# DeltaNet then Fourier mixing: odd heads' operands moved to the other half of the partitions, and the first merge done by halves

## The chip, the cores and the metric

The kernel runs on one core of a Trainium2 chip. The metric is device time in microseconds (us) of one execution; lower is better. Each comparison is between executions on the same chip. An execution more than 1.5 % above the fastest of its kernel counts as slow and is left out of the ratios. The kernel before has medians from 784 to 790 us in the different series, so kernels of different series are compared by their ratios, not by their times.

## The reference, cut to what matters

```python
# deltanet: batch 4, heads 8, positions 768, head dim 48
k_n = k / (np.linalg.norm(k, axis=-1, keepdims=True) + 1e-06)
for t in range(S):
    y[:, :, t] = np.einsum('bhd,bhde->bhe', q[:, :, t], state)
    v_old = np.einsum('bhde,bhd->bhe', state, kt)
    state = state + bt[..., None] * np.einsum('bhd,bhe->bhde', kt, vt - v_old)
# then, with x = y as (4, 768, 384):
mixed = np.real(np.fft.fft(np.fft.fft(x, axis=1), axis=2))
u = x + mixed
un = (u - mu) / np.sqrt(var + 1e-06)
out = u + np.maximum(un @ w_ch1, 0.0) @ w_ch2      # w_ch1 384 x 1536
```

The recurrence is computed in chunks of 64 positions, 48 chunks in all (12 per batch element). Within a chunk, R is the keys times the state, U = T B (V - R) with a triangular inverse T, S is the keys times U, and the state grows by S. T comes from inverting 32x32 blocks on VectorE and *merging* pairs of blocks to 64x64 with two small products.

## The kernel before, in the parts that matter

Four chunks form a quad, and two quads (eight chunks) are inverted together and are called a group here; a *load* is one quad's half of the merge. V is transferred for a whole chunk and four heads at once, so head u of a half of the heads always lies in the same 64 partitions:

```python
def fetch(Q, engs, dst, src):
    for c in range(QT):
        for hh in range(2):
            ...
            engs[hh].dma_start(out=dst[64 * hh:64 * hh + CH, c, :, 0:D],
                               in_=src[b, 4 * hh:4 * hh + 4, t0:t0 + CH, :].rearrange("h p d -> p h d"))
```

The second product of U and the merge therefore use only the diagonal tiles (rows and columns of the same half), two of the four 64x64 tiles of TensorE:

```python
for u in range(4):                       # U <- T B (V - R)
    for hh in range(2):
        pr = slice(64 * hh, 64 * hh + 64)
        mm(pu[pr, u], wt[pr, c, u], U[pr, u], True)
act.activation(U, pu, ACT.Copy)

class Merge:
    ...
    def taken(self, step):               # evacuates pj: four ACTIVATEs of 32x256
        for hh in range(2):
            for v in range(2):
                ...
                act.activation(dst, src, ACT.Copy, scale=-1.0 if step == 0 else 1.0)
    def diagonal(self, half):            # two copies of 32x512
        for hh in range(2):
            r = slice(64 * hh + W * half, 64 * hh + W * half + W)
            act.activation(self.wt[r, :, :, W * half:W * half + W], self.Z[r, self.ns], ACT.Copy)
```

After the inversion the first load is merged whole, before chunk 0 begins:

```python
M = Merge(0, 0)
for step in range(2):
    M.products(step, 0); M.products(step, 1); M.taken(step); M.diagonal(step)
scaled(0); run(masks(0)); scaled(1); run(masks(1))
...
for m in range(NCH): ... chain(m) ...
```

## Time and profile before

| | before |
|---|---|
| time, median of 3 (later of 4) | 788.09 us (788.83 us) |
| profiled span, mean granted clock | 784.7 us, 0.970 |
| PE busy | 699.9 us |
| ACT busy | 260.0 us |
| V transfers | 96 of 48 KB |

These are lines of the page of the kernel before: busy time by engine, the chain that ended last, two groups (busy us, mean ns, then idle time of the engine before them and what ended it), and V's transfers.

```profile
PE 699.9 (89%) x7640; PEld 513.0 (65%) x7640; DVE 379.4 (48%) x952; ACT 260.0 (33%) x634; POOL 58.7 (7%) x83
...
PE 48%; DVE 10%; ACT 5%; issue 3%; DMA 0%; SPq 0%; POOL 0%; POOLq 0%; DVEq 0%; ACTq 0%
...
L131 PEld LDWEIGHTS pc<-U,wt 64*64 64x64 f32 x768 | 34.0, 163 | 19.7 <-issue 10.3
...
V<-in_v_dram SPq DMA_DIRECT2D x96, 48.0 KB, 2.4
```

In all such lines ph and po are the MLP's two products (the last line of the reference) and unT and hT their inputs, evacuated by ACT; pj is the merge's product and wt its result, T B; pt, KQT and pg prepare later chunks.

PE is busy 89 %. pc<-U,wt is U's second product, which the change speeds up. Transfers (DMA, SPq) have no share of the chain; but its shares add up to only 66 %, as it could be followed back no further than 254 us, so it says nothing of the time before.

### The profile page before, as it was taken

Reading aid. Unit: us, or ns where it says so; the run is one execution under the profiler, and the core shown is the slowest. Engines: PE = TensorE matmul, PEld = TensorE weight load, DVE = VectorE, ACT = ScalarE, POOL = GpSimd, SP = SyncE. Lnnn points to the kernel's source line nnn. Section 1 sums busy time; section 2 is a strip of 40 time slices with the busy share of each in tenths; the row PEclk is TensorE's granted clock in tenths of the full one; section 3 lists DMA queues with packets and bytes.
Section 4 is the critical chain, followed back from the end, with each engine's and each line's share of the span. In section 5 each row is a group of like instructions: output and inputs, shape, how many; then the busy total and the mean of one; then the engine's idle time right before and its main releaser. Section 6 shows DMA issues by size and latency. Waiting matters only on the chain.

```text
span 784.7 us, 17842 instructions
## 1 busy us (share of the span) xinstructions
PE 699.9 (89%) x7640; PEld 513.0 (65%) x7640; DVE 379.4 (48%) x952; ACT 260.0 (33%) x634; POOL 58.7 (7%) x83
## 2 busy tenths in 40 slices
PE   5852799989988997999989998999999989999997
PEld 4531687867656765786666775776767666677684
DVE  2699766575992598245961119783111146100000
ACT  3741354227436404532152540315312121021120
POOL 8020000010000001010100001010000010100000
PEclk9999999989998999699999999899999999999999
DMA  8651033225320212001202101001000000000000
GB/s 189 163 113 31 7 85 57 46 74 123 87 69 9 38 32 43 16 10 25 50 6 42 32 2 42 1 1 32 12 12 11 12 11 1 20 1 20 11 11 20
DMA packets 82447, 30.75 MB, mean 39 GB/s; under 512 B 77392, under 2 KB 78928, under 8 KB 82368
## 3 DMA queue, kind: packets, MB, share of 16 engines
q1 hardware_dynamic: 78224, 22.31, 13.8%
q0 software_dynamic: 1968, 6.91, 2.7%
q8 instruction: 60, 0.98, 0.5%
q10 hardware_dynamic: 2176, 0.39, 0.3%
q14 instruction: 19, 0.16, 0.1%
HBM read 24.87 MB, written 4.72 MB: 38 GB/s over the span
## 4 chain that ended last, share of the span: by engine, by line
PE 48%; DVE 10%; ACT 5%; issue 3%; DMA 0%; SPq 0%; POOL 0%; POOLq 0%; DVEq 0%; ACTq 0%
PE ph L131 20%; PE po L131 15%; DVE X L131 3%; PE pc L131 3%; DVE A L131 2%; PE pf L131 2%; PE pj L131 2%; ACT A L131 2%; PE pb L131 2%; ACT wt L131 1%; PE pg L131 1%; PE py L131 1%; DVE sm L131 1%; DVE x L131 1%; PE pt L131 1%
## 5 line engine op out<-in xcount | busy, mean ns | idle before, releaser
L131 PE MATMUL ph<-unT,w 128*128 128x256 f32 x864 | 213.8, 395 | 4.5 <-ACT unT L131 2.0
L131 PE MATMUL po<-w,hT 128*128 128x384 f32 x576 | 202.2, 498 | 1.7 <-ACT KQT L131 0.7
L131 PEld LDWEIGHTS ph<-unT,w 128*128 128x128 f32 x864 | 160.3, 193 | 33.7 <-ACT hT L131 3.7
L131 PEld LDWEIGHTS po<-w,hT 128*128 128x128 f32 x576 | 105.7, 191 | 68.2 <-issue 1.5
L131 ACT ACTIVATE hT<-ph 128x256 f32<-128x256 f32 x144 | 54.9, 383 | 179.6 <-PE ph L131 179.3
L131 DVE TENSOR_TENSOR x<-x,po 128x384 f32<-128x384 f32 x24 | 13.2, 552 | 112.5 <-PE po L131 112.4
L131 ACT ACTIVATE U<-pc 128x192 f32<-128x192 f32 x48 | 15.9, 331 | 110.0 <-PE pc L131 98.4
L131 ACT ACTIVATE KQT<-pt 128x256 f32<-128x256 f32 (+1 forms) x82 | 32.0, 419 | 44.9 <-PE pt L131 44.3
L131 PEld LDWEIGHTS pc<-U,wt 64*64 64x64 f32 x768 | 34.0, 163 | 19.7 <-issue 10.3
L131 PE MATMUL pg<-KQT 48*64 48x64 f32 (+1 forms) x1024 | 41.7, 309 | 5.5 <-ACT KQT L131 4.4
L131 PEld LDWEIGHTS pg<-KQT 48*64 48x64 f32 x1024 | 32.1, 178 | 20.4 <-ACT KQT L131 11.2
L131 PE MATMUL pc<-U,wt 64*64 64x48 f32 x768 | 41.2, 253 | 4.7 <-DVE U L131 2.1
L131 DVE TENSOR_TENSOR st<-st,pc 128x192 f32<-128x192 f32 x44 | 15.3, 347 | 61.0 <-PE pc L131 56.8
L131 DVE TENSOR_TENSOR U<-V,pc 128x192 f32<-128x192 f32 x48 | 16.8, 350 | 53.1 <-PE pc L131 52.9
L131 DVE TENSOR_TENSOR A<-X 128x30 f32<-128x30 f32 (+14 forms) x120 | 41.0, 342 | 2.9
L131 DVE TENSOR_TENSOR X<-X,A 128x30 f32<-128x30 f32 (+14 forms) x120 | 39.5, 329 | 2.9
L131 DVE TENSOR_TENSOR x<-x,pb 128x193 f32<-128x193 f32 (+1 forms) x96 | 26.4, 346 | 23.1 <-PE pb L131 23.1
L716 POOL DMA_INDIRECT out_dram<-x,rows_hi x12 | 12.3, 1024 | 335.9 <-DVE x L131 179.9
L131 PE MATMUL pt<-pack,kp 128*128 128x128 f32 x96 | 24.4, 349 | 10.3 <-DMA pack<-k_pack 4.8
L131 PE MATMUL pt<-pack,qp 128*128 128x128 f32 x96 | 23.4, 341 | 11.0 <-DMA qp<-in_q_dram 11.0
L131 PE MATMUL pj<-Z,A 32*64 32x64 f32 x320 | 15.0, 257 | 19.9 <-DVE Z L131 19.6
L131 ACT ACTIVATE A<-pg 128x256 f32<-128x256 f32 (+1 forms) x72 | 25.4, 378 | 21.7 <-PE pg L131 16.6
(125 smaller groups left out, 840.2 us busy)
## 6 DMA issues: line engine op xcount, KB each, us to landing
qp<-in_q_dram SPq DMA_DIRECT2D x96, 48.0 KB, 2.4
V<-in_v_dram SPq DMA_DIRECT2D x96, 48.0 KB, 2.4
kp<-in_k_dram SPq DMA_DIRECT2D x80, 48.0 KB, 2.5
w<-in_moe_w_ch_dram SPq DMA_DIRECT2D x8, 384.0 KB, 3.2
w<-in_moe_w_ch_dram POOLq DMA_DIRECT2D x6, 384.0 KB, 6.4
x<-in_moe_w_ch_dram SPq DMA_DIRECT2D x6, 384.0 KB, 3.7
x<-in_moe_w_ch_dram POOLq DMA_DIRECT2D x4, 384.0 KB, 9.2
out_dram<-x SPq DMA_DIRECT2D x8, 192.0 KB, 2.0
```

The costliest lines, as they stand in the source:

```text
L131: ins = getattr(self.engine, name)(*args, **kwargs)
L716: nc.gpsimd.indirect_dma_start(out=out.rearrange("b s m -> (b s) m"), out_offset=bass.IndirectOffsetOnAxis(ap=rows_hi[:, i:i + 1], axis=0) ...
```

## The change

Its intent: keep the odd heads' V, R and T B in the other half of the partitions. Then an even and an odd head use different tiles, so U's second product and the merges can go round four tiles in place of two. Besides, the first load is merged by halves, with R of chunk 0 issued between, so that the chain starts earlier. The core of the diff:

```diff
-    def fetch(Q, engs, dst, src):
+    def fetch(Q, engs, dst, src, crossed=False):
...
+                if crossed:
+                    for e in range(2):
+                        h0 = 4 * (hh ^ e)
+                        engs[hh].dma_start(out=dst[64 * hh:64 * hh + CH, c, e::2, 0:D],
+                                           in_=src[b, h0 + e:h0 + 4:2, t0:t0 + CH, :].rearrange("h p d -> p h d"))
+                    continue
...
+            if i == 0:                               # in invert(): lengths of odd heads change sides
+                ...
+                dve.tensor_copy(odd, lns.rearrange("p g n -> p (g n)")[:, 1::2])
+                for hh in range(2):
+                    dve.tensor_copy(lns.rearrange("p g n -> p (g n)")[64 * hh:64 * hh + 64, 1::2],
+                                    odd[64 * (1 - hh):64 * (1 - hh) + 64])
...
-                        mm(self.pj[64 * hh:64 * hh + 64, hh, o:o + 64], ...
+                        p = 64 * hh if self.apart else 64 * (hh ^ w)
+                        mm(self.pj[half][p:p + 64, w, 64 * c:64 * c + 64], ...
...
+                    for ws in (slice(0, 2),) if self.apart else (slice(0, 1), slice(1, 2)):
+                        ...
+                        act.activation(dst[:, :, ws], src, ACT.Copy, scale=-1.0 if step == 0 else 1.0)
...
-                act.activation(self.wt[r, :, :, W * half:W * half + W], self.Z[r, self.ns], ACT.Copy)
+            for e in range(2):
+                o = 64 * (hh ^ e) + W * half
+                copy(self.wt[o:o + W, :, e::2, W * half:W * half + W],
+                     self.Z[r, QT * self.lh:QT * self.lh + QT, e::2])
...
-        for u in range(4):
-            for hh in range(2):
-                pr = slice(64 * hh, 64 * hh + 64)
-                mm(pu[pr, u], wt[pr, c, u], U[pr, u], True)
+        for j in range(2):
+            for e in range(2):
+                for hh in range(2):
+                    pr = slice(64 * (hh ^ e), 64 * (hh ^ e) + 64)
+                    mm(pu[64 * hh:64 * hh + 64, e, j], wt[pr, c, 2 * j + e], U[pr, 2 * j + e], True)
...
     first = invert(0, 1)
     advance(first, 4)
+    first_state(0)
...
-    M = Merge(0, 0)
-    for step in range(2): ...
+    M = Merge(0, 0, True)
+    M.products(0, 0); M.products(0, 1); M.taken(0); M.diagonal(0, 0); M.products(1, 0)   # on five lines
+    step = chain(0)
+    advance(step)
...
```

Not shown: the lists that fix what stands in which chunk of the first chain were rewritten too (the masks, for one, stood ahead of chunk 0 and now stand in chunks 1 and 3).

In number: V's transfers double to 192 of half the size, an evacuation has eight ACTIVATEs of 32x128 in place of four of 32x256, the diagonals of a load eight copies of 32x256 in place of four of 32x512, and PE's instructions stay as many.

## The prediction

> **What bounds the kernel now.** I read the page first, then the timeline of the first chain of chunks, then busy time per stage, then the timeline of a late stage. The page says that PE is busy 89% of 784.7 us, and its chain of work that ended last is PE for 48% with ph and po, the channel MLP, in front. That is an average over unlike stages, so I cut the span at the chain's own marks. The windows view (columns: stretch, length, then busy time of PE, PEld, DVE, ACT, POOL with instruction counts, granted clock, DMA share, GB/s):
>
> ```profile
> 80.60:88.30 7.70, 5.39 (x72) 4.30 (x72) 7.02 (x10) 4.66 (x11) 0.00 (x0) 1.00 0.00 0
> 88.30:142.30 54.00, 49.25 (x1077) 42.83 (x1075) 35.44 (x75) 25.07 (x59) 0.00 (x0) 1.00 0.29 60
> ...
> 256.00:330.00 74.00, 66.63 (x1018) 47.96 (x1010) 46.89 (x121) 29.42 (x76) 3.86 (x4) 0.88 0.17 32
> 330.00:633.00 303.00, 294.98 (x3239) 210.20 (x3237) 134.88 (x362) 89.60 (x222) 17.38 (x22) 0.98 0.09 19
> ```
>
> There are four stages that the change touches. Up to 80.6 us: loads and the inversion on DVE. 80.6 to 88.3: the first merge, alone. 88.3 to 142.3: chunks 0 to 11, a chain R -> U -> U's second product -> S -> state, with little to fill it. After that: the chain lies beside the MLP, and from 330 to 633 PE is busy 295 of 303 us. So before 142 us a latency counts, and after 330 us a saving of PE time counts. The timeline of chunk 1 shows the latency (columns: start, duration, engine, operation):
>
> ```profile
> 94.44 0.93 PEld L131 LDWEIGHTS pc<-U,wt 64*64 64x64 f32 x16 [0.64 <-DVE U L131]
> ...
> 95.46 0.93 PEld L131 LDWEIGHTS pj<-A 32*64 32x64 f32 x16
> ...
> 95.58 0.33 ACT L131 ACTIVATE U<-pc 128x192 f32<-128x192 f32 x1 [0.64 <-PE pc L131]
> 96.50 0.52 PEld L131 LDWEIGHTS pc<-U,kp 64*64 64x64 f32 x16
> ...
> 97.11 0.93 PEld L131 LDWEIGHTS pj<-A 32*64 32x64 f32 x16
> ```
>
> The two products that use two tiles (pc<-U,wt and pj) need 0.93 us for 16 weight loads, 58 ns each; S, which goes round four tiles, needs 0.52 us, 33 ns. In a late stage, by the same view:
>
> ```profile
> 540.67 0.32 PEld L131 LDWEIGHTS pc<-U,kp 64*64 64x64 f32 x16
> ...
> 542.54 1.01 PEld L131 LDWEIGHTS pj<-A 32*64 32x64 f32 x32 [0.55 <-ACT A L131]
> ...
> 543.73 1.53 ACT L131 ACTIVATE wt<-pj 32x256 f32<-32x256 f32 x4 [1.41 <-PE pj L131]
> ```
>
> There it is 0.32 us for 16 in four tiles, and 31.5 ns against 20 ns each. So the same change is worth 0.41 us per 16 early and about 0.2 us late.
>
> **What the Trainium skill says.** "TensorEngine Tiling (Array Packing)", section Tiling Modes: with 64x64 there are four tiles, and different tiles can run LdWeights and Matmul in parallel. The trace agrees: 33 ns against 58 ns. The same page, Performance Considerations: tiling speeds up TensorE but not PSUM evacuation, which may become the bottleneck. The trace is made for that: after 1.01 us of pj, ACT takes 1.53 us. "TensorE: Matmul & The Clock Gate", Part 1: the clock is halved while PE has been little used and full after sustained use. The page's clock row does not show it before 157 us, but durations do: the same 16 loads in 0.52 us at 96 us and 0.32 at 540. So I take early durations for the first chain. "DMA: Bandwidth & Descriptors", Rules for kernel authors: splitting a transfer over partition halves brings nothing, since all go through the same DMA engines; issue time is what counts. Here SyncE spends some 0.6 us on each 48 KB issue.
>
> **The change, part by part.**
>
> *U in four tiles.* One instruction group per chunk, 48 in all: 0.93 -> 0.52 us cold. A plain early chunk is now 3.92 us (chunk 2: R at 98.16 to R at 102.08); U's step and ACT's start follow it directly, so it could be 3.5.
>
> *Merging in four tiles, except the first load.* Each load has four groups of 16. In chunk 1, pj delays S by 0.55 us (0.93 against the 0.38 that S otherwise needs after ACT's start) and the next R by 0.40: chunk 1 lasts 4.88. With 0.52 each both delays vanish behind ACT and DVE. But the evacuation gets finer: eight ACTIVATEs of 32x128 instead of four of 32x256, and eight diagonal copies of 32x256 instead of four of 32x512. ACT's 32x256 takes 0.374 us and 32x512 0.628, so I estimate 0.12 us + 1 ns per element, 0.25 for 32x128. One taken(): 1.53 -> 2.0; the diagonals of a load: 2.54 -> 3.0. Per load +1.4 us of ACT, +15 us in all over eleven loads.
>
> *The first load by halves.* Now:
>
> ```profile
> 80.71 1.81 PEld L131 LDWEIGHTS pj<-Z,A 32*64 32x64 f32 x32 [17.11 <-issue]
> ...
> 82.75 1.53 ACT L131 ACTIVATE A<-pj 32x256 f32<-32x256 f32 x4 [18.30 <-PE pj L131]
> ...
> 87.89 1.28 ACT L131 ACTIVATE wt<-Z 32x512 f32<-32x512 f32 x2
> ...
> 89.54 0.96 PEld L131 LDWEIGHTS pc<-U,wt 64*64 64x64 f32 x16 [0.70 <-issue]
> ```
>
> After: pj half 80.7 to 81.65, ACT from 81.85: taken 1.05 and one diagonal pair 0.75, to 83.65; second pj half-step 82.95 to 83.9; R 83.9 to 84.4; U at 84.65; ACT taken 84.1 to 85.15, second diagonal 85.9 (the others on DVE by 86.0). The second product starts at about 86.0 instead of 89.54: 3.5 us. The rest of the merge (taken of the second half about 1.05 us after U, then 0.93 of pj) holds R of chunk 1 to about 89.2, against 93.28: 4.1 us.
>
> *Chunks 1 to 11.* Work that stood ahead of the chain is now inside it, and the whole of DVE's and ACT's order is fixed. I walked each chunk with the early durations:
> - chunk 1: DVE has masks (1.34) and a 2.0 us transpose between U and state, 1.35 more than the chain needs: 4.9 (was 4.87);
> - chunk 2: a whole load's merge, three output parts and a wait for taken(): 5.0 (was 3.92);
> - chunk 3: ACT has U 0.33, diagonals 3.0, split 1.0: about 3.9 (was 4.88);
> - chunk 4: 4.4 (was 4.06); odd chunks 5, 7, 9: five join steps of 0.48, an output add 0.55 and U on DVE: 4.4 each (were 5.82, 4.88, 5.82);
> - 6, 8: 3.7 each (were 3.98, 4.06); 10: 4.0 (3.98); 11: 2.5 (2.73).
> Sum: R of chunk 12 comes at 89.2 + 4.9 + 5.0 + 3.9 + 4.4 + 3 x 4.4 + 2 x 3.7 + 4.0 + 2.5 = 134.5, against 142.28. **First chain: -7.8 us.** I take -7.6 because of the loads below.
>
> *U after chunk 11.* 36 groups x 0.21 = 7.6 us of PE. PE idles little from 330 to 633, more from 142 to 330, and the two-tile groups partly interleave with py. I count 80%: **-6 us**.
>
> *Merges after chunk 11, eight loads.* PE saves 4 x 0.2 per load warm, but a step is a circle pj -> ACT -> pj. Late it is now 1.01 + 1.53 + about 0.2 = 2.8 us (pj at 542.54, 545.32, 548.10); after, 0.66 + 0.1 + 2.0 + 0.2 = 3.0. At 239 to 254 and 308 to 325 us ACT works through copies and takens almost without a pause, and gets 2.8 us more per pair of loads, while slow pj groups of 1.79 us become shorter. **+1.5 us**, uncertain by 2.
>
> *Twice as many V loads.* 96 issues become 192. From SyncE's timeline an issue of 256 rows takes 0.60 us and one of 128 rows 0.43 to 0.47, so each pair costs about 0.28 us more than one: 8 x 0.28 = 2.2 us per quad. At the start V takes 14.14 us of SyncE for 16 issues, and 4.5 more delay the query loads; queries are prepared by 64 us now and would be by 68.5, while DVE inverts until 77: hidden. V of quad 2 was issued from 103.2 to 111.8 and used at 117.86, some 3.5 us of slack; 2.2 more and an earlier use by 1.5 eat it. I count 0 to 2 us, 0.2 above.
>
> *Small parts.* The lengths' three extra copies (of 128x32) and the earlier first state are on DVE at a time when they can be slotted in: nothing.
>
> Sum: -7.6 - 6 + 1.5 = -12.1, so 788.1 -> 776.
>
> **The rivals.**
> 1. *ACT takes PE's place.* For: +1.4 us per load, and merges after 142 us are already a circle through ACT, where PE idles 4 to 7 us per merge (239 to 254, 308 to 325). Against: ACT is busy 33% overall and 90 of 303 us late. If each of the four later groups loses 2.5 us, late merges cost 10 instead of 1.5: 784.
> 2. *PE-bound throughout.* If the scheduler refills PE in the merges, they save 8 x 0.8 = 6.4 us and more where PE is cold, and U gives its full 7.6: 788 - 7.6 - 7.6 - 7 = 766. Against: the instruction order within the merge is set by the program, and the ACT circle is there in the trace.
> 3. *DVE or V's loads bound the first chain.* DVE is busy 35.4 of 54 us and would be at about 80% of the shorter stretch, in fixed order; a late V of quad 2 stops everything. Then the first chain gives only 4 to 5 us: 779.
> 4. *The clock.* Short stalls in a late stage can put PE at half clock for some microseconds (0.88 granted from 256 to 330); a cold window more or less is about 3 us either way.
>
> **Range and chances.** Rivals 1 and 3 push up, 2 down; they seldom come together, so 768 to 783. A gain of 2% needs 772.3, 3.7 us below my sum: it takes most of rival 2. I give 0.25. Slower by 2% would need a stall of 28 us that nothing here shows: 0.03.
>
> **What would show it.** pc<-U,wt at 0.52 us for 16 in the first chain and 0.32 late; pj at 33 and 20 ns per load; the first U product near 86 us and R of chunk 12 near 134.5; eight ACT records of 32x128 near 0.25 us per taken; ACT busy near 275 us. I am wrong if the four-tile order with rows 0, 1, 1, 0 runs at 58 ns, if U waits for V at chunk 6, or if the later merges move by more than 4 us.

## The result, and the profile after

| | before | after |
|---|---|---|
| time, median of 4 | 788.83 us | 795.95 us |
| range | 787.66 to 789.62 | 794.46 to 796.83 |
| ratio | | 1.009, 95 % interval 1.0065 to 1.0114 |
| profiled span, clock | 784.7 us, 0.970 | 795.1 us, 0.954 |
| PE busy | 699.9 us | 688.3 us |
| ACT busy | 260.0 us | 282.0 us |

A ratio here is the mean time of one kernel's fast runs over that of the other's of the same rounds, so not quite the ratio of the medians. The kernel became slower by 0.9 %, which lies outside my range of 768 to 783. The same lines of the page after:

```profile
PE 688.3 (87%) x7640; PEld 496.4 (62%) x7640; DVE 383.6 (48%) x971; ACT 282.0 (35%) x774; POOL 54.7 (7%) x83
...
PE 52%; DVE 22%; ACT 11%; DMA 5%; SPq 5%; issue 4%; POOL 0%; POOLq 0%; DVEq 0%; ACTq 0%
...
L131 PEld LDWEIGHTS pc<-U,wt 64*64 64x64 f32 x768 | 22.5, 161 | 26.1 <-DVE U L131 10.2
...
V<-in_v_dram SPq DMA_DIRECT2D x192, 24.0 KB, 2.2
```

PE's work did shrink: 11.6 us of matmul time and 16.6 us of weight loads, of which pc<-U,wt alone is 34.0 - 22.5 = 11.5. Yet the span grew by 10.4 us. The two chains' shares can't be compared as they stand, since the one before reaches back only to 254 us and the one after to the start. From 254 us on, added up from both traces, PE has 378 us of the chain before and 373 after, DVE 81 and 77, ACT 38 and 52, and SyncE's queue (SPq) 2 and 8: ACT and SyncE grew.

The windows view by stage says the same, first before, then after (stretch, length, busy us of PE, PEld, DVE, ACT, POOL, granted clock, DMA share, GB/s):

```profile
80.60:142.30 61.70, 54.64 (x1147) 47.13 (x1147) 42.46 (x85) 29.72 (x69) 0.00 (x0) 1.00 0.25 52
142.30:256.00 113.70, 100.11 (x1051) 76.12 (x1054) 74.69 (x202) 52.13 (x125) 7.65 (x10) 0.92 0.29 69
```

```profile
80.60:142.30 61.70, 45.91 (x1188) 38.75 (x1192) 44.73 (x89) 36.08 (x113) 0.00 (x0) 1.00 0.26 51
142.30:256.00 113.70, 91.21 (x922) 68.23 (x917) 73.69 (x202) 52.68 (x138) 7.65 (x10) 0.90 0.29 68
```

In the first chain PE is busy 8.7 us less in the same stretch, for only 41 more matmuls. In the second stretch PE gets through 129 matmuls fewer in the same time, so it fell behind there.

To find where, I subtracted the start of U's subtraction (U<-V,pc on DVE) of each chunk in the two traces. Only the steps of this difference matter:

| up to chunk | after - before, us | step | what lies there |
|---|---|---|---|
| 5 | -1.3 | | start and first chunks |
| 6 | -2.4 | -1.1 | |
| 7 | 0.0 | +2.3 | V of quad 2 comes late |
| 15 | -1.8 | -1.8 | |
| 16 | +3.5 | +5.3 | a PE pause at 183 us |
| 17 | +5.3 | +1.8 | merge of group 2; half clock for 13.7 us from 247.5 on, before for 6.8 from 245.8 |
| 24 | +8.0 | +2.8 | not traced |
| 30 | +7.6 | -0.4 | |
| 31 | +10.5 | +2.9 | merge of group 4, 412 to 428 us |
| 41 | +11.0 | +0.5 | |
| 47 | +9.5 | -1.4 | no merge, chain and MLP only |
| end | +10.4 | +0.9 | |

Five steps lose more than 1.5 us. Three of them (chunks 7, 16 and 31) and the start are read below; those at chunks 17 and 24 are not.

**The start.** Before, the last transpose of the inversion (Z) starts here:

```profile
78.57 2.02 DVE L131 STREAM_TRANSPOSE Z<-Y 128x1024 f32<-128x1024 f32 x1
```

After:

```profile
41.95 1.35 DVE L131 COPY ln<-sm 64x32 f32<-64x32 f32 x2
...
46.61 0.94 DVE L131 TENSOR_TENSOR V<-V,ln 128x768 f32<-128x768 f32 x1
...
81.11 2.02 DVE L131 STREAM_TRANSPOSE Z<-Y 128x1024 f32<-128x1024 f32 x1
...
88.27 1.16 PEld L131 LDWEIGHTS pc<-U,wt 64*64 64x64 f32 x16 [1.20 <-issue]
...
93.21 0.52 PEld L131 LDWEIGHTS pc<-U,wt 64*64 64x64 f32 x16 [0.64 <-DVE U L131]
93.81 0.51 PEld L131 LDWEIGHTS pj<-Z,A 32*64 32x64 f32 x16
```

Z is 2.5 us later. The lengths' copies (1.35 us), V's first scaling (0.94 us) and, not shown, the state's copy (0.36 us) run inside the inversion, where DVE has no gap to spare: together 2.65 us. From Z to U's first product it takes 88.27 - 81.11 = 7.2 us, against 89.54 - 78.57 = 11.0 before (89.54 is in the prediction's fence). So merging by halves gained 3.8 us and the small copies gave back 2.5.

**Chunk 6.** SyncE's timeline shows what an issue costs; first before, then after:

```profile
183.75 0.61 SPq L185 DMA_DIRECT2D V<-in_v_dram  x1
```

```profile
108.64 7.98 SPq L189 DMA_DIRECT2D V<-in_v_dram  x10
...
182.20 0.60 SPq L189 DMA_DIRECT2D V<-in_v_dram  x1
```

Half a transfer takes SyncE as long as a whole one, 0.60 against 0.61 us. V of quad 2 is therefore issued until 108.64 + 7.98 = 116.6. The last of these issues starts at 116.0, and with the page's median of 2.2 us to landing that piece is there at about 118.2 (an estimate; its own landing is not in the trace). Its scaling starts soon after, in the timeline after:

```profile
118.80 0.96 DVE L131 TENSOR_TENSOR V<-V,ln 128x768 f32<-128x768 f32 x1 [3.21 <-DMA kp<-in_k_dram]
120.81 0.52 PEld L131 LDWEIGHTS pc<-st,KQT 48*64 48x64 f32 x16 [3.05 <-DVE st L131]
```

DVE waits 3.2 us. The profile names kp, which shares the queue, as the last transfer awaited; by the times V is likelier, and e1 below, where V's issues end earlier, has no such wait. R of chunk 7 waits behind DVE.

**The pause at 183 us.** The timeline before:

```profile
182.97 1.46 ACT L131 ACTIVATE A<-pg 128x256 f32<-128x256 f32 x4 [0.68 <-PE pg L131]
...
184.45 1.21 ACT L131 ACTIVATE KQT<-pt 128x256 f32<-128x256 f32 x4
...
185.16 0.30 PEld L131 LDWEIGHTS ph<-unT,w 128*128 128x128 f32 x2 [0.63 <-ACT KQT L131]
...
185.86 1.02 ACT L131 ACTIVATE wtmp<-x 128x384 int32<-128x384 uint32 x2 [0.19 <-DMA x<-in_moe_w_ch_dram]
```

And after:

```profile
183.32 0.98 ACT L131 ACTIVATE wtmp<-x 128x384 int32<-128x384 uint32 x2 [2.81 <-DMA x<-in_moe_w_ch_dram]
...
185.66 1.21 ACT L131 ACTIVATE KQT<-pt 128x256 f32<-128x256 f32 x4
...
186.37 0.50 PEld L131 LDWEIGHTS ph<-unT,w 128*128 128x128 f32 x2 [3.62 <-ACT KQT L131]
```

wtmp<-x reads a piece of the second weight, which a transfer brings. Before it stands behind A and KQT; after it stands ahead of them and waits 2.8 us for its transfer. PE idles 3.6 us and then runs at half clock: the clock records have half speed from 186.0 to 192.8 us. Nobody changed these instructions. They are outside the part whose order the program fixes, and the two traces show that the order of ACT came out otherwise when the kernel was built.

**The merge of group 4.** Before, the diagonal copies on ACT and the MLP's second product (po):

```profile
405.33 1.91 ACT L131 ACTIVATE wt<-Z 32x512 f32<-32x512 f32 x3
...
411.57 5.43 PE L131 MATMUL po<-w,hT 128*128 128x384 f32 x16 [0.62 <-ACT unT L131]
```

After, with two rows of the windows view below:

```profile
412.08 2.96 ACT L131 ACTIVATE wt<-Z 32x256 f32<-32x256 f32 x7 [2.43 <-DVE Z L131]
...
414.07 0.45 PE L131 MATMUL pc<-U,wt 64*64 64x48 f32 x16 [1.45 <-DVE U L131]
...
417.20 0.31 PEld L131 LDWEIGHTS ptr<-pack,un 128*128 128x128 f32 x3 [1.39 <-ACT hT L131]
...
419.23 8.25 PE L131 MATMUL po<-w,hT 128*128 128x384 f32 x16 [0.62 <-ACT unT L131]
```

```profile
412.00:419.00 7.00, 3.02 (x57) 1.82 (x56) 3.29 (x6) 6.67 (x17) 0.00 (x0) 0.94 0.00 0
419.00:428.00 9.00, 8.77 (x48) 4.91 (x48) 0.18 (x2) 1.80 (x5) 0.00 (x0) 0.67 0.06 13
```

A copy of half the size takes two thirds of the time: 2.96 / 7 = 0.42 us against 1.91 / 3 = 0.64. Sixteen of them per group take 6.7 us where eight took 5.1. Ahead of the first po PE pauses for 1.45 us, for U on DVE, which stands behind two transposes there, and then for 0.75 and 1.15 us, for hT, which stands behind copies on ACT; before, one pause of 1.15 us was for hT. Then the clock falls: the same 16 po take 8.25 us in place of 5.43, with a mean granted clock of 0.67.

The loss of 2.9 us lies in this clock and not in the copies' own time: from U of chunk 30 on DVE to the first po it takes 419.23 - 413.68 = 5.55 us after, and 411.57 - 406.07 = 5.50 us before. In the 3.4 us ahead of the fall (414.7 to 418.1) PE was busy 1.25 us; in the two such stretches at this place before (406.3 to 413.1) it was busy 2.25 and 2.32 us, and the clock stayed full. Which of the pauses decided it is not shown.

If the clock is always full or half, as its records have it, the mean clock gives the time at half speed: 2 x (1 - 0.970) x 784.7 = 47 us before and 2 x (1 - 0.954) x 795.1 = 73 us after. The traces have no clock record before 157 and 155 us, so the first chain is not in this count.

### The profile page after: what moved, and what is told of

The parts are those of the page before. It is cut to its first block, busy times and chain, and to the rows that moved or that the text cites. A ratio compares the mean times of both kernels' runs of the same rounds, so it can differ in the third digit from the quotient of the medians.

```text
span 795.1 us, 18097 instructions
## 1 busy us (share of the span) xinstructions
PE 688.3 (87%) x7640; PEld 496.4 (62%) x7640; DVE 383.6 (48%) x971; ACT 282.0 (35%) x774; POOL 54.7 (7%) x83
## 3 DMA queue, kind: packets, MB, share of 16 engines
q1 hardware_dynamic: 79760, 22.31, 13.7%
## 4 chain that ended last, share of the span: by engine, by line
PE 52%; DVE 22%; ACT 11%; DMA 5%; SPq 5%; issue 4%; POOL 0%; POOLq 0%; DVEq 0%; ACTq 0%
PE ph L131 19%; PE po L131 15%; DVE A L131 5%; PE pc L131 5%; DVE X L131 4%; ACT wt L131 4%; SPq L189 3%; ACT A L131 3%; PE pf L131 3%; DVE w L131 3%; DVE x L131 2%; DMA qp<-in_q_dram 2%; PE pb L131 2%; PE py L131 2%; PE pg L131 2%
## 5 line engine op out<-in xcount | busy, mean ns | idle before, releaser
L131 PE MATMUL pg<-KQT 48*64 48x64 f32 (+1 forms) x1024 | 44.4, 318 | 5.1 <-ACT KQT L131 4.5
L131 PEld LDWEIGHTS pg<-KQT 48*64 48x64 f32 x1024 | 34.1, 183 | 19.9 <-ACT KQT L131 11.3
L131 PE MATMUL pc<-st,KQT 48*64 48x48 f32 x768 | 28.0, 260 | 14.9 <-DVE st L131 14.6
L131 PEld LDWEIGHTS pc<-st,KQT 48*64 48x64 f32 x768 | 21.2, 166 | 30.3 <-DVE st L131 19.7
L131 PE MATMUL pt<-pack,qp 128*128 128x128 f32 x96 | 23.9, 346 | 18.1 <-DMA qp<-in_q_dram 17.1
L131 PE MATMUL pc<-U,wt 64*64 64x48 f32 x768 | 30.8, 258 | 10.1 <-DVE U L131 4.9
L131 PEld LDWEIGHTS pc<-U,wt 64*64 64x64 f32 x768 | 22.5, 161 | 26.1 <-DVE U L131 10.2
```

Source lines behind the costliest of these rows:

```text
L131: ins = getattr(self.engine, name)(*args, **kwargs)
```

## The experiments

My theory after reading the traces: the wanted savings are there, and three side effects eat them. (1) V's doubled transfers; (2) the finer evacuation and diagonal copies on ACT; (3) the copies inside the inversion. The rivals: one of the three does it all; or the four tiles themselves are at fault; or, once it had shown up, the order of ACT at 183 us. All kernels gave correct results.

| run | kernel | ratio to before | 95 % interval | median, us |
|---|---|---|---|---|
| (after) | the change | 1.0090 | 1.0065 to 1.0114 | 795.95 |
| e1_vheads | after, V by heads | 1.0036 | 0.9973 to 1.0100 | 788.95 |
| e2_late | after, lengths, state, scaling late | 1.0147 | 1.0075 to 1.0218 | 797.18 |
| e3_dvediag | after, later diagonals on DVE | 0.9973 | 0.9930 to 1.0017 | 786.91 |
| e5_before_vsplit | before, V split in two | 1.0090 | 1.0050 to 1.0129 | 795.31 |
| e4_twotile | after, merges in two tiles | 1.0083 | 1.0012 to 1.0155 | 795.73 |
| e6_vheads_dvediag | e1 and e3 together | 0.9907 | 0.9876 to 0.9938 | 781.72 |
| e7_pool | e6, lengths and scaling on GpSimd | 0.9904 | 0.9871 to 0.9937 | 781.15 |
| e9_before_fine | before, finer evacuation | 1.0140 | 1.0103 to 1.0177 | 799.71 |
| e10_late | e6, lengths and scaling late | 0.9869 | 0.9837 to 0.9900 | 776.26 |
| e11_before_dvediag | before, later diagonals on DVE | 0.9939 | 0.9899 to 0.9979 | 779.41 |
| e12_twotile | e6, merges in two tiles | 0.9909 | 0.9874 to 0.9944 | 778.25 |
| e13_shared | e10, half of the evacuation on DVE | 1.0017 | 0.9986 to 1.0047 | 787.04 |
| e14_late_vpool | e10, V issued by GpSimd | 0.9899 | 0.9874 to 0.9925 | 778.69 |
| e15_after_vpool | after, V issued by GpSimd | 1.0085 | 1.0048 to 1.0122 | 791.12 |
| e16_before_wpool | before, second weight by GpSimd | 1.0101 | 1.0059 to 1.0143 | 797.12 |
| e17_vsplit_wpool | e16 with V split in two | 1.0097 | 1.0046 to 1.0148 | 795.28 |
| e18_after_wpool | after, second weight by GpSimd | 1.0094 | 1.0058 to 1.0130 | 797.11 |
| e19_late_wpool | e10, second weight by GpSimd | 0.9954 | 0.9909 to 0.9999 | 785.27 |

The series, each on one chip with its own runs of the kernel before: e1, e2, e3, e5 (788.70 us); e4, e6, e7, e9 (789.33); e10 to e13 (784.34); e14, e15 (786.30); e16 to e19 (789.75).

### V's transfers

**e1_vheads**: V one head at a time over four chunks: eight transfers of 48 KB per quad as before the change (sixteen of 24 KB in the quads whose positions jump in the middle).

```diff
-                if crossed: for e in range(2): ... two transfers per chunk and half
+        if crossed:
+            step = 2 if i == 1 else QT
+            for c in range(0, QT, step):
+                for u in range(4):
+                    for hh in range(2):
+                        ...
+                        h = 4 * (hh ^ (u % 2)) + u
+                        engs[hh].dma_start(out=dst[64 * hh:64 * hh + CH, c:c + step, u, 0:D], ...)
```

> The changed kernel with V loaded one head at a time over a whole quad (8 transfers of 48 KB per quad, 16 where the token offset breaks the quad), so 24 issues at the start instead of 32 and 8 or 16 per quad instead of 16. Theory A (the doubled V issues cost: each half-size issue took 0.6 us on SyncE, as a whole one did, and the chain shows SyncE and DMA with 5% each): chunk 6 no longer waits for V (about 2.3 us back), the wait for the weight transfer behind V and q near 180 to 187 us shrinks (2 to 5 us), total near 789. Rival B (DVE and ACT work is what was added): within 1 us of the changed kernel, about 795.

It came to 1.0036 with a wide interval, which contains both 1 and the change's 1.009. The trace is plainer: the scaling of quad 2 starts 3.3 us earlier, right behind U's subtraction, and the pause at 183 us is gone too.

```profile
115.51 0.96 DVE L131 TENSOR_TENSOR V<-V,ln 128x768 f32<-128x768 f32 x1
```

Against the kernel before, chunk 12 is 3.7 us early in place of 1.0, and chunk 24 1.2 us early in place of 8.0 late. At chunk 47 it is level with it again (+0.5), as the later merges take that lead.

**e5_before_vsplit**: the kernel before, with V's transfers split in two, heads not moved.

```diff
+                    for e in range(2):
+                        engs[hh].dma_start(out=dst[64 * hh:64 * hh + CH, c, e::2, 0:D],
+                                           in_=src[b, 4 * hh + e:4 * hh + 4:2, t0:t0 + CH, :]...)
```

> The kernel before with one part of the change alone: every V transfer split in two of two heads each (heads stay in their halves). Theory A: the slack of V in the first chain was 3.5 us and 16 issues of 0.6 us take 5 us more, so a stall of 1 to 3 us at chunk 6 and later waits; total 791 to 795. Rival: issue time is hidden, 788 to 789.

The split alone costs 0.9 %. But its timeline is level with the kernel before up to chunk 15 (+0.2 us) and loses 6 us in chunk 16 alone (2.2 of them come back by chunk 17), where ACT has the changed order: wtmp<-x ahead of A and KQT, waiting 3.0 us, and PE pausing 3.8 us.

```profile
185.50 0.98 ACT L131 ACTIVATE wtmp<-x 128x384 int32<-128x384 uint32 x2 [3.00 <-DMA x<-in_moe_w_ch_dram]
```

So the loss might be this order and not SyncE's time in general. Two pairs of runs were made for that.

**e15_after_vpool** and **e14_late_vpool**: V's transfers issued by GpSimd, in the changed kernel and in e10 (below).

```diff
-        fetch(Q, (nc.sync, nc.sync), vals[Q], v, True)
+        fetch(Q, (nc.gpsimd, nc.gpsimd), vals[Q], v, True)
```

> The changed kernel with nothing altered but the queue of its V transfers: the same 192 of 24 KB, issued by GpSimd instead of SyncE. If SyncE's issue time and its order are the cost (V before q, k and the weights in one line), as much comes back as in e1, about 788 to 789. If it is the number of transfers or their bytes in flight, it stays at 795 or gets worse[...].

> e10 with V's transfers on GpSimd's queue. In e12, and likely in e10, the chain still shows SyncE's V issues just before the group whose quad breaks at the token offset, which has 16 of them. If that is the rest of V's cost, 2 to 4 us faster than e10 (about 773 on the same chip); if V is hidden there, the same; slower if GpSimd's issue is late for the first scaling.

SyncE was freed of 192 issues, and the stall of chunk 6 went (3.6 us from U to U in e15), as did the pause at 183 us. The ratio stayed at 1.0085, because other places lost: 2.7 us between chunks 14 and 16 and 2.5 in the late merge. (This trace is of the fastest of four executions and ends 3.1 us behind the kernel before.) In e15 ACT has the changed order as well, but wtmp<-x finds its transfer landed and does not wait: the order costs where the transfer comes later than its turn. e14 is within the interval of e10. These two leave the question open.

**e16_before_wpool** to **e19_late_wpool**: the second weight's twelve transfers issued by GpSimd. I compared the instruction orders before the runs: with this edit ACT has wtmp<-x ahead of A and KQT in all four, so the order no longer differs between the kernel with V whole (e16) and the one with V split (e17).

```diff
-                nc.sync.dma_start(out=stages[p % 2], in_=w2v[:, p])
+                nc.gpsimd.dma_start(out=stages[p % 2], in_=w2v[:, p])
```

> The kernel before with the second weight's twelve transfers issued by GpSimd in place of SyncE. It is the control for the next run; ACT's copies of the words now stand ahead of A<-pg and KQT<-pt here too. (a) If the order alone costs, and the words land no earlier, it loses like the V split: about 1.007 to 1.009 of before. If the words land in time because SyncE isn't in their way: within 0.3 % of before, no PE pause over 1.5 us near 183 us.

> The same with V's transfers split in two. (a) If the place of ACT's copies and their wait was the whole cost of the split: within 0.3 % of the control above, where the split alone cost 0.9 % against its own. (b) If SyncE's time on V's issues is the cost in general: 0.6 to 0.9 % above the control, with chunk 16 some 5 us later than in the control.

> The changed kernel with the second weight's transfers on GpSimd. (a): the PE pause of 3.5 us at 182.9 goes and with it its half clock: about 5 us less than after, 1.002 of before (0.999 to 1.005). (b): 1.007 to 1.010, as after. The pause for V at chunk 6 (about 3 us) must stay in either case.

> The best version so far (V by heads, diagonals on DVE, lengths and first scaling behind the inversion; 0.987 of before) with the second weight's transfers on GpSimd. It had no pause near 183 us, so (a) expects no gain: 0.984 to 0.990; a gain of over 0.4 % would say that SyncE's time counts there too, as (b) has it.

e16 lost 1.0 % without any change to V, heads or merges; it also moved transfers to GpSimd, so the loss isn't the order's alone for certain. e17, with V split, is equal to it (1.0097 against 1.0101). With equal order the split costs the kernel before nothing that these runs resolve. e19 says the same from the other side: the best version had no pause here, gets one with this edit (ACT waits 3.3 us, PE idles 3.6), and goes from 0.9869 to 0.9954. My expectation for it was wrong, as I had not counted the new order against it. What doesn't fit a simple price per wait: e17 waits only 1.2 us where e16 waits 2.9, and ends level. And e18 was expected at 1.002 and is at 1.0094. Its pause at 183 us is indeed gone and chunk 16 is 4.7 us earlier than in the changed kernel, but it then runs 37.5 us at half clock from 245 us on, where the changed kernel has 13.7, and from chunk 16 to 20 it loses 9.3 us more than that kernel does. The traced execution is the slowest of its six (801.03 us, median 797.11), so its half clock is more than e18 usually has. A wait removed ahead of an unstable stretch doesn't have to arrive at the end.

### The evacuation

**e9_before_fine**: the kernel before, with eight ACTIVATEs of 32x128 per evacuation and diagonal copies of 32x256; nothing else.

```diff
-                    act.activation(dst, src, ACT.Copy, scale=-1.0 if step == 0 else 1.0)
+                    for w in range(2):
+                        act.activation(dst[:, :, w:w + 1], src[:, :, w:w + 1], ACT.Copy, scale=...)
...
-                act.activation(self.wt[r, :, :, W * half:W * half + W], self.Z[r, self.ns], ACT.Copy)
+                for e in range(2):
+                    act.activation(self.wt[r, :, e::2, W * half:W * half + W], self.Z[r, self.ns, e::2], ACT.Copy)
```

> The kernel before with the finer evacuation alone: every 32x256 ACTIVATE of taken() as two of 32x128 and every 32x512 diagonal copy as two of 32x256, no four-tile product. Theory C: ACT alone, some 1.7 us more per load, lengthens each merge and stops hT behind it; 5 to 9 us slower than before, with more half-clock time. Rival (it is the four-tile products that idle PE and cool its clock): at most 3 us slower.

It costs 1.4 %, the largest cost of any part of the change that was tried alone, for 11 us more of ACT work (271.1 busy against 260.0) on an engine that is busy 34 %. It has no pause at 183 us. It loses most right behind the merge of group 2: +1.1 us at chunk 17, +5.8 at chunk 20, +7.8 at chunk 24, with half clock for 20.5 us from 247.7 on where the kernel before has 6.8. At the end of the chain it is +9.9. In the merge of group 4 it loses only 0.3, so this cost doesn't fall in the same merge each time.

**e3_dvediag**: the changed kernel with the diagonal copies of the later merges on DVE.

```diff
-                M.diagonal(step, 0)
-                M.diagonal(step, 1)
+                M.diagonal(step, 0, dve.tensor_copy)
+                M.diagonal(step, 1, dve.tensor_copy)
```

> The changed kernel with the diagonal copies of the merges after the first chain on DVE instead of ACT. Theory C (the finer evacuation makes ACT hold up the MLP's hT and unT, PE stands idle at the later merges, and its clock is halved after: 71 us of half clock after 157 us against 44 before): PE's wait near 412 to 418 us goes, the cold window at 418 to 425 goes, 4 to 6 us back in all, about 790. Rival A: no more than 1 us, as DVE is on the path there as well.

It takes back 1.2 %. From chunk 16 to 17 (group 2) it gains 3.9 us on the kernel before, where the changed kernel lost 1.8, and from 30 to 31 (group 4) it gains 2.9 where that lost 2.9; at group 3 it gives 4.8 back, with 23.9 us at half clock. The merge of group 4 shows how it gains. DVE does all sixteen copies in 4.74 us, ACT is free for hT and unT, and po keeps its full speed (8 in 2.85 us):

```profile
408.74 4.74 DVE L131 COPY wt<-Z 32x256 f32<-32x256 f32 x16
...
410.62 2.85 PE L131 MATMUL po<-w,hT 128*128 128x384 f32 x8
```

**e11_before_dvediag**: the same edit in the kernel before.

> The kernel before with its later diagonal copies on DVE and nothing else. If the mend of e3 only takes back what the change had added, 787 to 789. If ACT's share in the merges was a cost of the kernel before too, 3 to 6 us faster (783 to 786), and then the change's own ideas are worth only the rest of e6's 7.6 us.

It gains 0.6 %: the diagonals on ACT were a burden before the change already. From U of chunk 30 to the first po takes 2.1 us in e3 and 2.4 in e11, against 5.5 before and after and 5.3 in e9. So e3's 1.2 % is not the price of the finer copies alone; about half of it could be had without the change.

**e4_twotile** and **e12_twotile**: merges in two tiles again (U's product stays in four), with four ACTIVATEs per evacuation; in the changed kernel and in e6.

```diff
-                        p = 64 * hh if self.apart else 64 * (hh ^ w)
+                        p = 64 * hh
...
-                    for ws in (slice(0, 2),) if self.apart else (slice(0, 1), slice(1, 2)):
+                    for ws in (slice(0, 2),):
```

> The changed kernel with all merges on two tiles again, so that one ACTIVATE of 32x256 evacuates what two of 32x128 did; U keeps its four tiles, the diagonal copies stay fine on ACT. If the finer taken() costs more than the four-tile pj saves, this is 1 to 4 us faster than the changed kernel (about 793); if the pj saving counts, it is 2 to 5 us slower (about 799).

> e6 with all merges on two tiles and evacuated by four ACTIVATEs of 32x256. In the changed kernel this made no difference (e4). With the diagonals off ACT, either the circle through ACT still sets the pace and fewer, larger ACTIVATEs win 1 to 3 us (about 779), or the four-tile pj counts and it is 2 to 4 us slower (about 785).

Each is equal to its parent (1.0083 and 1.0090; 0.9909 and 0.9907). So the merges gain nothing from four tiles that these runs resolve (their intervals are 0.007 and 0.0035 either way), and the rival "the four tiles are at fault" falls for the merges; U kept its four tiles in both. In the prediction's terms the saving on pj and the dearer evacuation cancel. That leaves the diagonal copies as the part of (2) that can cost. No run makes them alone finer, so this is by elimination.

**e13_shared**: e10 with half of each later evacuation on DVE.

```diff
+                        if both and hh == 1:
+                            dve.tensor_scalar(dst[:, :, ws], src, -1.0 if step == 0 else 1.0, None, op0=ALU.mult)
+                        else:
```

> e10 with half of each later taken() on DVE, so that the evacuation of a merge step takes some 1.1 us on each of two engines instead of 2.2 on one. If the circle pj, evacuation, pj sets the pace of the later merges, 2 to 4 us faster than e10 (about 776); if not, the same.

It loses 1.5 % against e10. DVE's order has the 16 diagonal copies, the evacuations and V's scaling in one row, and DVE is busy 85 us in the four merge windows against 56. Sharing PSUM evacuation over both engines hurt here, where the second one stands in the chain.

### The start

**e2_late**: the changed kernel, with the lengths' exchange, first state and first scaling behind the inversion.

```diff
-    first_state(0)                    # behind advance(first, 4)
...
     strict[0] = True
+    put_off.pop()()                   # the lengths' exchange
+    first_state(0)
     M = Merge(0, 0, True)
```

> The changed kernel with the first group's exchanged lengths, the first state and the first scaling of V put behind the inversion in program order. Theory B: these DVE instructions (0.94 us of scaling, some 1.6 us of copies and waits, 0.4 us of state copy) stand in the DVE-bound inversion from 34 to 83 us and delay it by 2.5 us, so Z's transpose starts near 78.6 instead of 81.1 and the first second product of U near 86.5 instead of 88.3; total about 793 to 794. Rival (the inversion is late for another reason, the query loads behind V): Z stays at 81.

A failure of design. Z came at 78.65, as wished, but the first state's matmuls now stood ahead of the merge in PE's order, R waited for them, and U's first product was at 88.9. The ratio, 1.0147, is not resolved from the change's 1.0090.

**e7_pool**: e6 with the lengths' exchange and the first scaling on GpSimd.

```diff
+                eng = nc.gpsimd if G > 1 else dve
+                eng.tensor_copy(odd, ...)
...
-            dve.tensor_tensor(vf, vf, ...)
+            (dve if Q else nc.gpsimd).tensor_tensor(vf, vf, ...)
```

> e6 with the first group's exchange of lengths and the first scaling of V on GpSimd, which has nothing to do between 45 and 83 us. Theory B: they delayed the DVE-bound inversion by 2.2 of its 2.5 us, so Z's transpose comes at 79.0 instead of 81.1 and the first second product of U at 86.2 instead of 88.3, and the total is 2 us below e6. (e2 couldn't tell: there the first state's products stood ahead of the merge in PE's order and ate the gain.) Rival: GpSimd and DVE share their way into memory, the inversion steps get longer, nothing is gained.

No gain: Z still came at 81.12. The scaling takes GpSimd 2.3 us, and the masking work that GpSimd has to do at that time starts only behind it; while GpSimd is busy, a DVE step that otherwise takes 0.22 us takes 1.17:

```profile
45.78 1.17 DVE L131 TENSOR_TENSOR w<-w,A 128x60 f32<-128x60 f32 x1
```

This agrees with the Trainium skill, "SBUF — State Buffer", section Who interferes with whom: a DVE instruction with two SBUF inputs contends with a GpSimd instruction that reads SBUF, and the later one is blocked. The work moved away came back as a lock.

**e6_vheads_dvediag** is e1 and e3 together.

> The changed kernel with both mends that helped alone: V by heads (e1, about 7 us back) and the later diagonal copies on DVE (e3, about 8 us back). If the two costs lie at different places (V at chunks 6 and 15 to 16, ACT at the merges of the later groups), they add: about 780 to 782, 1% below the kernel before. If they share one wait, 786.

0.9907: both repairs together bring the change below the kernel before.

**e10_late** is e6 with the lengths' exchange and first scaling on DVE behind the inversion, the first state left where it was.

```diff
     first = invert(0, 1)
     advance(first, 4)
     first_state(0)
...
     strict[0] = True
+    put_off.pop()()                   # the lengths' exchange; the first scaling follows it
     M = Merge(0, 0, True)
```

> e6 with the exchange of lengths and the first scaling of V put behind the inversion on DVE, while the first state stays ahead. Theory B as in e2, with its flaw removed: Z's transpose near 79.0 us instead of 81.4, U's first second product near 86.2 instead of 88.5, total 2 us below e6 (about 779.5). If Z comes early and the product doesn't, something else holds it.

Z came at 80.00 and the first product at 87.14, 1.4 us before e6's. At 0.9869 (776.26 us against 784.34) this is the best version found, ahead of both kernels. With it the change is worth 1.3 %, of which the kernel before could have had 0.6 % from the diagonals alone.

## Why the prediction was wrong

**The reading of the page: incomplete.** The prediction quotes "PE for 48%" without saying that this chain reaches back only to 254 us, so that the first chain of chunks isn't in it. The stages were cut by other views, and its sums don't rest on this.

**PE's savings: right.** U's second product took 0.52 us in the first chain and 0.32 late, as predicted; pj about 32 ns per load early. From chunk 41 to 47, where no merge or new load interferes, the changed kernel gains 1.4 us in six chunks, 0.24 us each, against 0.21 predicted. But the step "U after chunk 11 ... I count 80%" took this for all 36 chunks. In the chunks from 17 to 40 no such gain can be seen in the differences; it is lost among larger waits.

**The first load by halves: mechanism right.** I predicted 3.5 us from Z to the first product and 3.8 were measured.

**"Small parts ... can be slotted in: nothing": wrong.** They cost 2.65 us of DVE in the inversion and moved Z by 2.5. The stage up to 80.6 us is bound by DVE, as I wrote myself on "loads and the inversion on DVE"; I should have asked where the instructions are placed in its order. e10 gets 1.4 us of it back.

**"Twice as many V loads": wrong in its size and incomplete.** I took an issue to cost 0.43 to 0.47 us at half size; it costs 0.60, the same as a whole one. The transfers of 0.43 and 0.47 us in SyncE's timeline are of a table and of a weight, not of V. The term was "0 to 2 us, 0.2 above" and measured 2.3 at chunk 6, which e1 removes. I named that wait as the sign of error ("if U waits for V at chunk 6"). The second cost was not foreseen at all: 5.3 us at 183 us, from an ACT order that changed with V's split. e5 shows the loss there without the rest of the change, e16 and e19 show such waits and losses without any new split, and e17 beside e16 shows no further loss from the split. Why the order flips when the kernel is built was not traced.

**"First chain: -7.8 us": wrong.** R of chunk 12 came at 141.11, not 134.5: 1.2 us gained. Of the 6.6 missing, 2.9 are there at R of chunk 1 (92.05, not 89.2; the late Z is 2.5 of them) and 2.6 come in chunk 6 (6.33 us, not 3.7). The remaining 1.1 are the rest of the walk: chunks 3, 5, 7 and 9 were 0.4 to 0.7 us longer than I had them, chunks 1, 2 and 4 0.3 to 0.6 shorter. e10, without those two at full size, has chunk 12 4.8 us early.

**"Merges after chunk 11: +1.5 us, uncertain by 2": wrong.** Each ACTIVATE was sized a little low, 0.27 us for 32x128 (predicted 0.25) and 0.42 for the 32x256 diagonal copy (0.374), so ACT's busy time grew by 22.0 us and not by 15. But the step that failed is another: I priced ACT's extra time as a delay in the circle pj -> ACT -> pj. On that circle it cancels against pj (e4, e12). The loss fell on the MLP: around the diagonal copies PE pauses, in part for hT, and the clock then slows what follows. e9 measured the finer evacuation alone at 1.4 %, some 11 us. My rival 1 had named ACT with 2.5 us per group; the merge of group 4 lost 2.9, but by the clock. Rival 4 put the clock at 3 us; it was 26 us more at half speed, though part of this is time in which PE had little to do anyway.

**What stays open.** The parts don't add up. By e5 and e9 the side effects cost 0.9 and 1.4 %, and the whole change costs only 0.9, so its wanted part would be worth about 1.4 %. Yet e12, which has the four-tile U and the early start, is only 0.3 % ahead of e11, which lacks them, with intervals that overlap. The stretches from 245 to 330 us, where the clock switches several times, turn small shifts into 3 to 10 us (9.3 in e18's trace), and a sum of single effects can't be trusted across them. No run has the four-tile U or the early start alone, and none holds ACT's order in the later merges fixed while the copies change.

## What to carry to other kernels

Before counting PE time as saved, list every instruction that the new layout makes smaller: a transfer or a copy of half the size cost 100 % and 66 % of the whole one here, and it fell on the engines that feed PE. If an engine evacuates results for TensorE, put copies that nobody is waiting for elsewhere: here that gained 0.6 and 1.2 % (e11, e3), and pauses of PE of 0.75 to 3.6 us were followed by half clock, which cost 2.8 us behind the merge of group 4. And compare the instruction order of each engine after any change of transfers: an untouched instruction that moved ahead of others cost 5 us.

## What the Trainium skill lacked or had wrong

- "DMA: Bandwidth & Descriptors", Rules for kernel authors: that small transfers are mostly overhead agrees (2.2 us to landing for 24 KB, 2.4 for 48 KB). Apart from a table of sequencer cycles per instruction, the page has no time for an issue on the issuing engine: here 0.60 us on SyncE for a strided transfer of V of 24 KB and 0.61 for 48 KB, so the number of V's transfers counts and not their size.
- "TensorEngine Tiling (Array Packing)", PSUM Bottleneck: right that the copy may become the bottleneck. Its advice to use both ScalarE and VectorE cost 1.5 % here (e13), as VectorE was in the chain; and it doesn't say that the halves land in smaller pieces, with eight ACTIVATEs of 0.27 us for four of 0.37.
- "TensorE: Matmul & The Clock Gate", Part 1, gives an idle window of about 3.4 us as what halves the clock. Here it fell behind 3.4 us in which PE was busy 1.25 us and no pause was longer than 1.15 us (414.7 to 418.1), and 16 po then took 8.25 us in place of 5.43; with 2.25 us busy in 3.4 (406.3 to 409.7 before the change) it stayed full. Its section "A second HAM failure mode: psum-queue depth-cycling" does say that short idling between groups makes the clock swing; a figure for how much idling is enough is lacking.
- No page has the effect of build order: the same ACTIVATEs placed ahead of others made ACT wait 2.8 to 3.3 us for a transfer and PE pause for 3 to 3.8 us (after, e5, e16, e19), and nothing where the transfer had landed (e15).
